# Attention and down-projection in 64-row tiles: one TensorE mode for scores and sums

## The chip, the cores and the metric

The kernel runs on one core of a Trainium2 chip. The metric is device time in microseconds (us) of one execution, the median of several runs. One execution was also taken with the hardware profiler; every line of a profile shown here comes from such an execution.

## What is computed

```
scores = z @ z.T / S                       # per batch, S = 3008, d_qk = 64
attn   = max(scores, 0) ** 2
x      = u * (attn @ v)                    # D = 256
h      = x @ w_in                          # 256 -> 2048
out    = (h * sigmoid(1.702 * h)) @ w_out  # 2048 -> 256
```

There are 8 batches of 3008 rows. Inputs and output are float32 in DRAM; the kernel computes in float16 with float32 sums.

## The kernel before

**Tiles.** A batch has 24 row blocks of 128 (NJ, the last one half full, 64 rows, called SREM) and six chunks (NCH) of 512 columns, the last one 448 wide. The transposed z (ZT) holds the 64 values of d_qk twice, on partitions 0 to 63 and on 64 to 127, so that two score matmuls of 64 rows can run side by side on the two halves of the array, each into its own PSUM bank.

**Scores.** `scores` handles units. A unit (i, jp) is two row blocks against one chunk: two 64-row matmuls into a two-bank PSUM tile sc (L198), one ScalarE activation (Relu, L210, or L207 for a narrow unit) to float16, one VectorE squaring (L224, L215, L208) into a tile a. Since scores are symmetric, units below the diagonal are not computed but taken from transposing DMAs on SP's queue (tt, ad; L230, L217). `take(b, n)` issues the next n units of a queue; the tables SCHED (batches 1 to 7), SCHED0 (batch 0) and TAIL say at which step of which chunk how many are taken, and units are made about one chunk before they are used. Units are taken in groups of three in most places.

**Attention.** `attend(b, i)` sums over 23 full row blocks and the half block for chunk i: o[c] += V[j, c].T @ a[j], for the two column halves c of D. Each step is a 128-row matmul of 512 columns (L281). Chunks 0 and 1 of batch 0 alternate between both c (`both`); all others do c = 0 first and then c = 1, with one half-block step, in which both c get a 64-row matmul, between them (or where AT says). When a sum is complete, `gate` multiplies it by the transposed u on VectorE (L290, into xt).

**Feed-forward.** `up_group` does two 128-row blocks of w_in: four matmuls into a two-bank tile hg (L314), gelu on ScalarE (L322), a scaling on VectorE (L323) into gt. `down(b, k, s, h)` does half of the 16 row blocks of w_out for 128 output rows: eight matmuls of 256 columns into yp (L337); after a pair of row blocks ScalarE evicts it (y, L343) and issues the store. 19 up groups (LAGY) are issued among the steps of chunks 4 and 5 (HEAD). The other 29 alternate with one `down` each; the remaining downs come last, and among them the score units of the next batch's chunk 0 (TAIL).

**Loads.** u comes in by four DMAs on GpSimd's queue per chunk (`load_u`, L168); the first waits until VectorE has transposed the chunk that had the buffer (`turn_u`, L175, at step 12 of a chunk, TURN). V comes in on SP's queue and is cast on GpSimd (L153); z of the next batch also goes through GpSimd (L129 to L132).

**Order and buffers.** The order of each engine's instructions is the order in which the program writes them; semaphores are set where data or buffers require it. [...] ps2 has 3 buffers of two banks (sc, hg, zp), ps1 has 2 of one bank (o, yp).

Of the kernel before, what the change touches and what calls it, by code (L numbers as in the profile page):

```python
# [9 lines left out]
F32 = mybir.dt.float32  # L10
F16 = mybir.dt.float16
P = 128
# [3 lines left out]
def kernel(  # L16
# [16 lines left out]
    B, S, D = u.shape  # L33
# [29 lines left out]
    pu = ctx.enter_context(tc.tile_pool(name="pu", bufs=2))  # L63
    pa = ctx.enter_context(tc.tile_pool(name="pa", bufs=1))
    pw = ctx.enter_context(tc.tile_pool(name="pw", bufs=2))
    ps2 = ctx.enter_context(tc.tile_pool(name="ps2", bufs=3, space=bass.MemoryType.PSUM))
    ps1 = ctx.enter_context(tc.tile_pool(name="ps1", bufs=2, space=bass.MemoryType.PSUM))
    ET = mybir.EngineType
    ctx.enter_context(tc.manual_schedule(engines={ET.PE, ET.Pool, ET.SP, ET.DVE, ET.Activation}))

# [3 lines left out]
    dve.memset(nil, 0.0)  # L74

    ZT, V16, UQ, UT, XT, unit, TT = {}, {}, {}, {}, {}, {}, {}

    def warm_up(n):

# [30 lines left out]

    def first_zt(g):
        z2 = ZT["st"][:, g * CB:(g + 1) * CB]
        zp = ps2.tile([P, CB, P], F16, name="zp", tag="ps2")
        for k in range(CB):
            pe.transpose(zp[:, k, :], z2[:, k, :, :], ident)  # L115
        zt = ZT[0][:, g * CB:(g + 1) * CB, :].rearrange("d n p -> d (n p)")
        nb = CB if g < NCH - 1 else CB - 1
        dst = zt[:, :nb * P].rearrange("d (p n) -> d n p", n=nb)
        if g == 0:
            act.activation(dst, zp[:, :nb, :], AF.Copy, scale=1.0)  # L120
        else:
            dve.tensor_copy(dst, zp[:, :nb, :])  # L122
        if nb < CB:
            dve.tensor_copy(zt[:, nb * P:], zp[:, nb, :])
# [124 lines left out]
        return TT[b, cj, i][:, :, g, :]  # L249


    def attend(b, i, both=False, at=0):


        n = width(i)
        js, cs = list(range(NJ - 1)), range(2)
        own = i * CB
        if b == 0 and i == 3:
            js = js[own:-CB + 1] + js[:own] + js[-CB + 1:]
        elif b and i < NCH - 2:  # L260
            js = js[own:own + 2] + js[own + CB:-CB + 1] + js[own + 2:own + CB] + js[:own] + js[-CB + 1:]
        if both:
            order = [(c, j) for j in js[:-CB] for c in cs] + [(c, j) for c in cs for j in js[-CB:]]
            order.insert(-CB, (None, NJ - 1))
        else:
            order = [(c, j) for c in cs for j in js]
            order.insert(NJ - 1 - at, (None, NJ - 1))
        first = [next(k for k, s in enumerate(order) if s[0] in (c, None)) for c in cs]
        final = [max(k for k, s in enumerate(order) if s[0] in (c, None)) for c in cs]
        acc = {}  # L270

        def step(k):
            half, j = order[k]
            a = weights(b, i, j)
            for c in cs:
                if half not in (c, None):
                    continue
                if k == first[c]:
                    acc[c] = ps1.tile([P, CH], F32, name="o", tag="ps1")
                h = slice(c * SREM, (c + 1) * SREM) if half is None else slice(0, P)  # L280
                pe.matmul(acc[c][:, :n], V16[b][h, j, c, :], a[h], start=k == first[c], stop=k == final[c])  # L281
            for c in cs:
                if k == final[c]:
                    gate(c)

        def gate(c):
            ut = UT[b, i][:, c].rearrange("p q t -> p (q t)")
            x = XT[b, i]
            if i < NCH - 1 or b % 2:
                dve.tensor_tensor(x[:, c, :n], acc[c][:, :n], ut[:, :n], ALU.mult)  # L290
            else:
                dve.tensor_tensor(x[:, c, :LFULL], acc[c][:, :LFULL], ut[:, :LFULL], ALU.mult)
                dve.tensor_tensor(XT[b + 1, i][:, c, LAST:], acc[c][:, LFULL:n], ut[:, LFULL:n], ALU.mult)

        XT[b, i] = XT.get((b, i)) or pa.tile([P, NCC, CH], F16, name="xt", tag="xt", bufs=8)
        if i == NCH - 1 and b % 2 == 0:
            XT[b + 1, i] = pa.tile([P, NCC, CH], F16, name="xo", tag="xo")
        return [lambda k=k: step(k) for k in range(len(order))]


    GT, Y = {}, {}

    def blocks(b):

        return [(i, CH if i < NCH - 1 or b % 2 else LFULL) for i in range(NCH)]
# [22 lines left out]
    def down(b, k, s, h):  # L328
# [12 lines left out]
        if h == 1 and (s % 2 == 1 or s == ns - 1):  # L341
            s0 = s - s % 2
            act.activation(Y[b, k][:, s0:s + 1, :], yp[:, :s % 2 + 1, :], AF.Copy, scale=1.0 / FSC)  # L343
        r0 = b * S + i * CH
        full = min(n, S - i * CH) // P
        final = b == B - 1 and k == NCH - 1
        if h == 1 and (s == ns - 1 or final and s % 2 == 1):
            s0 = s - 1 if final else 0
            act.dma_start(
                out[r0 + s0 * P:r0 + min(full, s + 1) * P].rearrange("(n p) c -> p n c", p=P),  # L350
                Y[b, k][:, s0:min(full, s + 1), :],
            )
        if h == 1 and s == ns - 1 and full < ns:
            for h_, bb in enumerate((b, b - 1)):
                (act if b == B - 1 else pool).dma_start(
                    out[bb * S + S0:(bb + 1) * S], Y[b, k][h_ * SREM:(h_ + 1) * SREM, full, :],
                )


    LAGY = 2 * NFG + 3  # L360
    HEAD = {NCH - 2: (14, 4), NCH - 1: (0, 4)}

    def pieces(b, i):

# [6 lines left out]
    def split(lst, sizes):  # L371
# [6 lines left out]

    TAIL = {3: 3, 7: 3, 11: 3, 15: 3}
    SCHED = {
        0: {4: 3, 16: 3, 28: 3, 40: 3},
        1: {8: 3, 23: 3},
        2: {8: 3, 23: 3},
        3: {23: 3},
        4: {8: 3},
        5: {},
    }
    AT = {0: -5, 4: NJ - 1 - 8}  # L390


    TURN = {(True, i): 12 for i in range(1, NCH - 1)}
# [3 lines left out]
    SCHED0 = {  # L397
        0: {0: 1, 6: 2, 14: 2, 22: 2, 30: 2, 38: 2},
        1: {0: 2, 8: 2, 15: 2, 22: 2, 30: 2, 38: 2},
        2: {0: 2, 8: 2, 23: 3, 34: 3},  # L400
        3: {8: 3, 23: 3},
        4: {1: 3, 12: 3, 23: 3},
        5: {0: 1},
    }
    AT0 = {4: NJ - 1 - 12}
    HEAD0 = {NCH - 2: (28, 4), NCH - 1: (2, 3)}

    queue = []

    def take(b, n):  # L410
        if n:
            group = [queue.pop(0) for _ in range(n)]
            scores(b, group)
# [22 lines left out]

    for b in range(B):
        nup = NCH * NFG
        sched, head_at, half_at = (SCHED, HEAD, AT) if b else (SCHED0, HEAD0, AT0)
        head = 0  # L440
        for i in range(NCH):
            for n, step in enumerate(attend(b, i, b == 0 and i < 2, half_at.get(i, 0))):
                if b == 0 and i == 0 and n == 5:
                    load_u(0, 0)
                if b == 0 and i == 0 and n in FIRST_ZT:
# [4 lines left out]
                    if k + 2 < NCH:  # L450
                        load_u(b, k + 2)
                take(b, sched[i].get(n, 0))
                h0, hn = head_at.get(i, (n + 1, 1))
                if head < LAGY and n >= h0 and (n - h0) % hn == 0:
                    up_group(b, head)
                    head += 1
                step()
# [18 lines left out]
        for q in range(head, nup):  # L476
# [4 lines left out]
            up_group(b, q)  # L481
            if q >= LAGY:
                down(b, *downs.pop(0))
        for n in range(len(downs)):
            if more:
                take(b + 1, TAIL.get(n, 0))
            down(b, *downs[n])


# [28 lines left out]
```

## Time and profile before

| | |
|---|---|
| median of 3 runs | 1251.93 us (1250.12 to 1258.75) |
| the profiled execution's own time | 1250.78 us |
| its span, first to last instruction | 1248.8 us |
| TensorE matmuls (PE) | 1239.4 us busy, 7575 matmuls |
| ScalarE (ACT) | 754.2 us busy |
| VectorE (DVE) | 628.5 us busy |
| GpSimd (POOL) | 233.3 us busy |
| granted TensorE clock | 1.000 over the span |

A line of the chain in order of time has the start in us, the length in us, the engine, the tile written, the line of the code and the number of instructions. A line of the timeline has start, length, engine, line, operation, tile written and tiles read, the shape (rows * columns of the weights for a matmul), the number of instructions that follow each other, and in brackets how long the engine was idle before and what ended that. PEld is TensorE's weight load; a q after an engine's name means its queue or sequencer. [...] matmuls that follow each other overlap in these rows; the distance between starts is what one costs.

### The profile page before, as it was taken

To read this page: it belongs to the slowest core of one execution; us is meant where nothing else is said; L and a number is where in the kernel's file an instruction comes from. 1 tells how busy PE (TensorE), PEld (TensorE's weight loads), DVE (VectorE), ACT (ScalarE), POOL (GpSimd) and SP (SyncE) were. 2 spreads that over 40 slices of the span, in tenths; PEclk is the share of its full clock that TensorE was granted. 3 is DMA by queue.
4 is the path that set the end of the run, shared out by engine and by line. 5 is a ranking of instruction groups with operands and counts; after the bars stand their busy time and mean duration, and the time that the engine had idled before them with its cause. 6 is when DMAs were issued, how large, how long until landed. Compare 5 with 4: busy or idle time off the path is not lost.

```text
span 1248.8 us, 19199 instructions
## 1 busy us (share of the span) xinstructions
PE 1239.4 (99%) x7575; PEld 682.6 (55%) x7575; DVE 628.5 (50%) x901; ACT 754.2 (60%) x829; POOL 233.3 (19%) x333
## 2 busy tenths in 40 slices
PE   8999999999999999999999999999999999999998
PEld 3345764466544675446754467444674446734566
DVE  7665445544455445554454544655445454464431
ACT  5776674566745667366673666745666456664663
POOL 4224202221022210223102230022211222000000
PEclk9999999999999999999999999999999999999999
DMA  9937279622886228852397524965239552493001
GB/s 229 185 66 171 71 167 181 126 68 69 186 167 127 69 85 191 162 106 68 95 192 155 106 76 99 205 130 107 98 102 197 120 113 84 117 196 74 1 35 68
DMA packets 370394, 151.75 MB, mean 122 GB/s; under 512 B 312864, under 2 KB 363936, under 8 KB 370304
## 3 DMA queue, kind: packets, MB, share of 16 engines
q1 hardware_dynamic: 311840, 96.38, 36.3%
q0 software_dynamic: 33440, 29.37, 12.0%
q10 hardware_dynamic: 25024, 24.78, 6.0%
q8 instruction: 59, 0.97, 0.3%
q14 instruction: 31, 0.25, 0.1%
HBM read 60.29 MB, written 24.64 MB: 68 GB/s over the span
## 4 chain that ended last, share of the span: by engine, by line
PE 97%; DVE 1%; issue 1%; ACT 1%; DMA 0%; SPq 0%; ACTq 0%; DVEq 0%
PE o L281 38%; PE yp L337 27%; PE hg L314 26%; PE sc L198 6%; DVE a L224 1%; ACT rl L210 0%; DMA zf<-in_z_dram 0%; DVE zst L109 0%; DVE ut L175 0%; DVE xt L290 0%; DVE ZT L122 0%; PE zp L115 0%; ACT y L343 0%; SPq L95 0%; ACTq L210 0%
## 5 line engine op out<-in xcount | busy, mean ns | idle before, releaser
L322 ACT ACTIVATE gf<-hg 128x1024 f32<-128x1024 f32 (+1 forms) x384 | 385.9, 1006 | 232.4 <-PE hg L314 221.5
L323 DVE TENSOR_SCALAR gt<-gf 128x1024 f16<-128x1024 f32 (+1 forms) x384 | 278.1, 725 | 326.7 <-ACT gf L322 324.4
L210 ACT ACTIVATE rl<-sc 128x1024 f16<-128x1024 f32 x311 | 299.5, 1025 | 161.2 <-PE sc L198 160.0
L337 PE MATMUL yp<-W,gt 128*128 128x256 f16 x3008 | 371.1, 273 | 0.0
L281 PEld LDWEIGHTS <-V 128*128 128x128 f16 (+1 forms) x2304 | 213.1, 98 | 280.0 <-issue 43.3
L314 PE MATMUL hg<-xt,W 128*128 128x512 f16 (+1 forms) x1408 | 354.6, 374 | 0.0
L337 PEld LDWEIGHTS <-gt 128*128 128x128 f16 x3008 | 292.1, 98 | 90.6 <-issue 11.1
L281 PE MATMUL o<-a,V 128*128 128x512 f16 (+2 forms) x1244 | 297.0, 373 | 0.8 <-DVE a L224 0.8
L224 DVE TENSOR_TENSOR a<-rl 128x1024 f16<-128x1024 f16 x276 | 192.2, 697 | 170.3 <-ACT rl L210 170.2
L168 POOL DMA_DIRECT2D uq<-in_u_dram x188 | 126.1, 678 | 629.0 <-DVE ut L175 619.3
L281 PE MATMUL o<-tt,V 128*128 128x512 f16 x920 | 219.0, 379 | 0.9 <-DVE xt L290 0.9
L314 PEld LDWEIGHTS <-W 128*128 128x128 f16 x1536 | 149.7, 98 | 125.6 <-issue 1.4
L153 POOL CAST V<-vst 128x512 f16<-128x512 f32 x96 | 67.9, 746 | 143.8 <-PE o L281 116.1
L198 PE MATMUL sc<-ZT 64*128 64x512 f16 (+1 forms) x692 | 93.4, 373 | 0.9 <-DVE ZT L122 0.8
L343 ACT ACTIVATE y<-yp 128x512 f32<-128x512 f32 x96 | 56.4, 588 | 50.8 <-PE yp L337 50.3
L290 DVE TENSOR_TENSOR xt<-o,ut 128x512 f16<-128x512 f32 x80 | 54.7, 685 | 36.7 <-PE o L281 36.7
L175 DVE STREAM_TRANSPOSE ut<-uq 128x1024 f32<-128x1024 f32 (+1 forms) x48 | 58.4, 1216 | 0.2
L198 PEld LDWEIGHTS <-ZT 64*128 64x128 f16 x692 | 24.1, 94 | 58.3 <-issue 45.7
L215 DVE TENSOR_TENSOR a<-rl 128x1024 f16<-128x1024 f16 x35 | 24.2, 692 | 45.2 <-ACT rl L210 44.9
L207 ACT ACTIVATE rl<-sc 128x512 f16<-128x512 f32 x35 | 20.9, 597 | 41.6 <-PE sc L198 41.6
L281 PE MATMUL o<-ad,V 128*128 128x512 f16 x140 | 41.6, 379 | 0.0
L314 PE MATMUL hg<-xo,W 128*128 128x512 f16 x128 | 32.8, 379 | 0.0
(28 smaller groups left out, 92.3 us busy)
## 6 DMA issues: line engine op xcount, KB each, us to landing
out_dram<-y ACTq DMA_DIRECT2D x40, 512.0 KB, 2.9
vst<-in_v_dram SPq DMA_DIRECT2D x39, 512.0 KB, 4.5
uq<-in_u_dram POOLq DMA_DIRECT2D x156, 128.0 KB, 2.9
tt<-a SPq DMA_TRANSPOSE x230, 3.2
uq<-in_u_dram POOLq DMA_DIRECT2D x32, 112.0 KB, 3.1
vst<-in_v_dram SPq DMA_DIRECT2D x8, 384.0 KB, 4.4
out_dram<-y ACTq DMA_DIRECT2D x7, 384.0 KB, 3.1
zst<-in_z_dram POOLq DMA_DIRECT2D x7, 368.0 KB, 6.0
```

The source lines that it names most:

```text
L153: pool.tensor_copy(V16[b][:, n0:n0 + VB, k, :].rearrange("p n (q c) -> p n q c", c=QW), vst.rearrange("p n (q k c) -> p n q k c", k=NCC, c ...
L168: eng.dma_start(uq[k * QW:(k + 1) * QW, :n // QW].rearrange("t q k c -> t q (k c)"), src[:, :, cs])
L175: dve.transpose(ut[:, :, :n // QW, :].rearrange("p k q t -> p q k t"), UQ.pop((b, i))[:, :n // QW])
L198: pe.matmul(sc[:, r, :m * P], zt[h, 2 * kp + r, :], zt[h, (qi + 1) * CB - m:(qi + 1) * CB, :], start=True, stop=True,)
L210: act.activation(rl, sc, AF.Relu, scale=csc)
L224: dve.tensor_tensor(a, rl, rl, ALU.mult)
L281: pe.matmul(acc[c][:, :n], V16[b][h, j, c, :], a[h], start=k == first[c], stop=k == final[c])
L314: pe.matmul(hg[:, e, :n], W1[:, c, ff * P:(ff + 1) * P], XT[b, i][:, c, :n], start=(c == 0), stop=(c == NCC - 1),)
L322: act.activation(gf[:, :, :n], hg[:, :, :n], AF.Gelu_apprx_sigmoid, scale=1.0 / FSC)
L323: dve.tensor_scalar(g, gf[:, :, :n], FSC, None, ALU.mult)
L337: pe.matmul(yp[:, s % 2, :], GT[b, k, ff // CB][:, ff % CB, s * P:(s + 1) * P], W2[:, ff, :], start=(ff == 0), stop=(ff == NFF - 1),)
L343: act.activation(Y[b, k][:, s0:s + 1, :], yp[:, :s % 2 + 1, :], AF.Copy, scale=1.0 / FSC)
```

## The change

- Attention of chunks 2 to 4 in batch 0 and of chunks 0 to 4 in all others no longer uses 128-row matmuls. Each step is a pair of 64-row matmuls: rows 0 to 63 of block j for c = 0 and rows 64 to 127 for c = 1, each into its own bank. After all blocks and the half step, the tiles swap: rows 0 to 63 go to c = 1 and rows 64 to 127 to c = 0. Chunk 5 stays with 128 rows, and its half step is now its first.
- The last two row chunks of the down projection (chunks 4 and 5, in all batches but the last) are done by the new `down64` in the same way: pairs of 64-row matmuls of 256 columns, each row tile at another block of output rows, then swapped. With four blocks of output rows it uses two PSUM tiles and one swap, with three (chunk 5 in batches 0, 2, 4, 6) three tiles and two swaps. All its y evictions come at its end.
- At each swap a bank passes from one row tile to the other. `post` puts a wait for the last pair on GpSimd's queue, and `behind` makes the next pair wait for that.
- Score units are taken one at a time, spread over the steps, two at the swap (step NJ).
- The 19 early up groups are all issued in chunk 5.
- PSUM: ps2 has 2 buffers and ps1 has 4; zp moves to ps1. The store becomes a function of its own.

```diff
-    ps2 = ctx.enter_context(tc.tile_pool(name="ps2", bufs=3, space=bass.MemoryType.PSUM))
-    ps1 = ctx.enter_context(tc.tile_pool(name="ps1", bufs=2, space=bass.MemoryType.PSUM))
+    ps2 = ctx.enter_context(tc.tile_pool(name="ps2", bufs=2, space=bass.MemoryType.PSUM))
+    ps1 = ctx.enter_context(tc.tile_pool(name="ps1", bufs=4, space=bass.MemoryType.PSUM))
...
+    TOP, LOW, FULL = slice(0, SREM), slice(SREM, P), slice(0, P)
+    def post(last):
+        sig = pool.nop()
+        for m in last:
+            tc.add_manual_dep(sig.ins, m.ins.name, SYNC, reason="row tiles of one bank")
+        return sig
+    def behind(sig, m):
+        tc.add_manual_dep(m.ins, sig.ins.name, SYNC, reason="row tiles of one bank")
...
+        half = [(0, TOP, NJ - 1), (1, LOW, NJ - 1)]
         if both:
-            order = [(c, j) for j in js[:-CB] for c in cs] + [(c, j) for c in cs for j in js[-CB:]]
-            order.insert(-CB, (None, NJ - 1))
+            order = [[(c, FULL, j)] for j in js[:-CB] for c in cs] + [[(c, FULL, j)] for c in cs for j in js[-CB:]]
+            order.insert(-CB, half)
+        elif i == NCH - 1:
+            order = [half] + [[(c, FULL, j)] for c in cs for j in js]
         else:
-            order = [(c, j) for c in cs for j in js]
-            order.insert(NJ - 1 - at, (None, NJ - 1))
+            order = [[(0, TOP, j), (1, LOW, j)] for j in js] + [half] + [[(1, TOP, j), (0, LOW, j)] for j in js]
...
+        acc, turn = {}, NJ if order[-1][0][1] != FULL else -1
         def step(k):
+            done = []
+            for m in order[k]:
+                c, h, j = m
+                if (k, m) == first[c]:
+                    acc[c] = ps1.tile([P, CH], F32, name="o", tag="ps1")
+                ins = pe.matmul(
+                    acc[c][:, :n], V16[b][h, j, c, :], weights(b, i, j)[h],
+                    start=(k, m) == first[c], stop=(k, m) == final[c],
+                )
+                if k == turn:
+                    behind(acc["sig"], ins)
+                done.append(ins)
+            if k == turn - 1:
+                acc["sig"] = post(done)
...
+    def down64(b, k):
+        ns = blocks(b)[k][1] // P
+        shift, per = (2, 2) if ns == CB else (1, 1)
+        order = [(s, (s + shift) % ns, ff) for s in range(ns) for ff in range(NFF)]
+        turns = [32] if ns == CB else [16, 32]
+        last = {s // per: n for n, o in enumerate(order) for s in o[:2]}
+        yp, sigs = {}, {}
+        def step(n):
+            s0, s1, ff = order[n]
+            done = []
+            for s, h in ((s0, TOP), (s1, LOW)):
+                new = s // per not in yp
+                if new:
+                    yp[s // per] = ps1.tile([P, 2, D], F32, name="yp", tag="ps1")
+                ins = pe.matmul(
+                    yp[s // per][:, s % per, :], GT[b, k, ff // CB][h, ff % CB, s * P:(s + 1) * P], W2[h, ff, :],
+                    start=new, stop=n == last[s // per],
+                )
+                if n in turns:
+                    behind(sigs[n], ins)
+                done.append(ins)
+            if n + 1 in turns:
+                sigs[n + 1] = post(done)
+            if n == len(order) - 1:
+                y = Y[b, k] = pw.tile([P, CB, D], F32, name="y", tag="y")
+                for m in range(ns // per):
+                    act.activation(y[:, m * per:(m + 1) * per, :], yp[m][:, :per, :], AF.Copy, scale=1.0 / FSC)
+                store(b, k, ns - 1)
...
-    HEAD = {NCH - 2: (14, 4), NCH - 1: (0, 4)}
+    HEAD = 2
-    TAIL = {3: 3, 7: 3, 11: 3, 15: 3}
+    TAIL = {1: {n: 1 for n in (3, 12, 44, 54)}, 2: {n: 1 for n in (4, 25, 34, 43)}}
     SCHED = {
-        0: {4: 3, 16: 3, 28: 3, 40: 3},
-        1: {8: 3, 23: 3},
-        2: {8: 3, 23: 3},
-        3: {23: 3},
-        4: {8: 3},
+        0: {n: 1 for n in (1, 4, 7, 11, 28, 30, 33, 36, 39, 43)} | {NJ: 2},
+        1: {n: 1 for n in (4, 9, 34, 40)} | {NJ: 2},
+        2: {n: 1 for n in (4, 9, 34, 40)} | {NJ: 2},
+        3: {n: 1 for n in (38,)} | {NJ: 2},
+        4: {n: 1 for n in (2,)} | {NJ: 2},
         5: {},
     }
...
-        2: {0: 2, 8: 2, 23: 3, 34: 3},
-        3: {8: 3, 23: 3},
-        4: {1: 3, 12: 3, 23: 3},
+        2: {n: 1 for n in (0, 3, 7, 11, 30, 34, 38, 42)} | {NJ: 2},
+        3: {n: 1 for n in (4, 9, 34, 40)} | {NJ: 2},
+        4: {n: 1 for n in (0, 3, 6, 9, 12, 32, 36)} | {NJ: 2},
         5: {0: 1},
...
+        if more:
+            while downs[0][0] < NCH - 2:
+                down(b, *downs.pop(0))
+            for k in range(NCH - 2, NCH):
+                turns, steps = down64(b, k)
+                at = {n: 3 - len(turns) for n in turns} | TAIL[len(turns)]
+                for n, step in enumerate(steps):
+                    take(b + 1, at.get(n, 0))
+                    step()
```

## The prediction

> **What bounds the kernel now.** I read the engine shares first, then the chain that ended last, then that chain in order of time, then ScalarE's, VectorE's and GpSimd's timelines of the same stretch.
>
> ```profile
> PE 1239.4 (99%) x7575; PEld 682.6 (55%) x7575; DVE 628.5 (50%) x901; ACT 754.2 (60%) x829; POOL 233.3 (19%) x333
> PE 97%; DVE 1%; issue 1%; ACT 1%; DMA 0%; SPq 0%; ACTq 0%; DVEq 0%
> ```
>
> TensorE is busy 99% of the span and is 97% of the chain, and no wait of it in the list of waits exceeds 1.2 us in total. So only TensorE's own slots count: what makes it stream less, or stand still. The chain in order of time shows what a slot is:
>
> ```profile
> 307.96 0.86 PE hg L314 x4
> 308.82 3.49 PE yp L337 x32
> ...
> 316.56 0.75 PE sc L198 x6
> 317.31 3.60 PE yp L337 x32
> ```
>
> Four 512-wide matmuls take 0.86, so 0.216 each; 32 of 256 take 3.49, so 0.109 each. Six score matmuls (64 rows, two row tiles side by side) are three pairs and should take 0.65; they take 0.75, and the 32 matmuls after them 3.60 instead of 3.49. So entering 64-row mode costs 0.10 and leaving it 0.11: 0.107 a switch. In the order of instructions I counted neighbours with different row counts: 262 switches before. 262 x 0.107 = 28 us is what the modes cost now.
>
> ```profile
> 345.08 2.86 ACT L210 ACTIVATE rl<-sc 128x1024 f16<-128x1024 f32 x3 [1.56 <-PE sc L198]
> ...
> 347.97 0.69 DVE L224 TENSOR_TENSOR a<-rl 128x1024 f16<-128x1024 f16 x1 [0.23 <-ACT rl L210]
> 348.58 1.24 DVE L175 STREAM_TRANSPOSE ut<-uq 128x1024 f32<-128x1024 f32 x1
> ...
> 348.75 0.82 PE L198 MATMUL sc<-ZT 64*128 64x512 f16 x6
> 349.18 2.85 ACT L210 ACTIVATE rl<-sc 128x1024 f16<-128x1024 f32 x3 [1.24 <-PE sc L198]
> ...
> 350.11 2.62 POOL L168 DMA_DIRECT2D uq<-in_u_dram  x4 [18.46 <-DVE ut L175]
> ```
>
> ScalarE starts 0.43 after a score unit's first matmul. Three evictions in a row take 2.86, one 1.02: they follow each other every 0.91, and a unit's PSUM is free about 0.06 after its own 1.02. The squaring starts 0.03 later, the transposition of u 0.61 after the squaring, the four DMAs for the next u 0.29 after its end.
>
> [...] here four such (zp, 17.86 to 18.08) took 0.22, so 55 ns. [...] it is a run of four.
>
> **The change, part by part**, against the profiled execution (1250.8; its span 1248.8).
>
> *Modes.* The streaming work stays: 128 rows in one matmul or two 64-row tiles in a pair take one slot. In the built order I count 46 switches. 216 x 0.107 = 23.1 us gained. The doubled loads and matmuls lie in the pair's slot: score pairs already load two tiles of weights under the preceding pair. 512-wide pairs give an instruction every 54 ns, as yp does now. The 832 pairs of 256 need one every 27 ns, zp's rate in a short run: I take 0.109. It cannot be less, since streaming fills it; at twice the rate seen per instruction in yp it would be 0.218 and cost 91 us.
>
> *Swap signals.* post() puts a wait for TensorE's last pair on GpSimd's queue and lets TensorE's next weight load wait for it. 56 are added: 38 in attention, 18 in down64. Where the queue is free the way there and back is short: a CAST on GpSimd is seen to start some 0.1 after the matmul it waits for ends. The matmul ends 0.38 after its start, 0.1 to GpSimd, 0.1 back and a load make 0.6; the two score units placed at the turn fill 0.22 + 0.43 = 0.65. Nothing. But GpSimd works in order, and in chunks 1 and 2 of batches 1 to 7 the signal stands behind the four u DMAs. Counting from the score unit at step 9:
>
> - VectorE: 0.43 + 1.02 + 0.03 (squaring) + 0.61 + 1.24 (transposition) + 0.29 = 3.62, first u DMA;
> - GpSimd's sequencer runs ahead of its engine, but not by four: in the two lines below (its timeline, and the rows of L129) four such DMAs begin at 229.38, and the semaphore wait that stands behind them ran at 230.8, 1.4 later. So 5.0, and 5.1 back at TensorE;
> - TensorE: 0.22 for the unit, 15 steps of 0.216, two units 0.43: it is there at 3.9.
>
> ```profile
> 229.38 2.70 POOL L168 DMA_DIRECT2D uq<-in_u_dram  x4 [12.58 <-DVE ut L175]
> ...
> L129 POOLq EVENT_SEMAPHORE  x1: 17/17/17, 230.8 to 230.8; - x1
> ```
>
> Stall 1.1 to 1.2, which nothing covers: TensorE waits in order, and all matmuls are behind. 14 x 1.15 = 16.1. In batch 0 chunk 3 is alike (1.15), and in chunk 2 the unit stands at step 11, two steps nearer: 1.6. Together 18.9. Before, the same DMAs were late too, but nothing stood behind them.
> In down64 with three row blocks (batches 0, 2, 4, 6) each of two swaps has one unit as cover: there at 0.109 + 0.216 = 0.33, back at about 0.5. 8 x 0.2 = 1.6. The other ten have two units: nothing. What else stands ahead of signals on GpSimd (the casts of V after chunk 5, the u DMAs of the up projections, the load of W2 before batch 0's chunk 4) is over microseconds earlier.
>
> *PSUM.* ps2 goes from three buffers to two, so a unit must wait for the eviction of the last but one. In chunk 0 (from step 24) units stand at 24, 24, 28, 30, 33, 36, 39, 43, with the first at 0 us:
> - evictions start at 0.43 and 1.34, end at 1.45 and 2.36;
> - step 28 is reached at 1.30 and waits to 1.51: 0.21. Step 30 is reached at 2.16 and waits to 2.42: 0.26. From there 0.87 lie between units against 0.91 for an eviction: 0.04 each, three times.
> So 0.6 a batch, 4.2 in all. Earlier in the chunk, the evictions of y (0.60, 0.42 for a 256-wide one) and the out DMA (0.38 on ScalarE's queue) now come together at the end of down64, just ahead of the units at steps 1, 4 and 7. Odd batches before it: the y pair and the DMA keep ScalarE from 0.31 to 1.85 after the last pair, the unit of step 1 is out at 2.87, step 7 wants its buffer at 2.06: 0.9, three times. Even ones, about 0.3, four times. 4.0.
> ps1 has four buffers, but down64 with three blocks takes one more tile, so chunk 0's second accumulator gets the bank of the block's first y. ScalarE still evicts the unit of step 43 (0.43, next start 1.34), then y (0.42): free at 1.8, wanted at five steps of 0.109 + 0.22 = 0.76. 1.04 x 4 = 4.1.
>
> *Order.* Chunk 5 now begins with its half step, and in batch 0 that needs the unit issued at the same step: 0.43 + 1.02 + 0.03 + 0.69 + 0.05 = 2.2 against 0.2, so 2.0 lost once; the 0.9 of waits of o for xt goes, since o has four buffers. 1.1. Up heads in chunk 5: one each 2 or 3 steps of 0.189 plus 0.86, at least 1.24; ScalarE needs 1.0 for each: hidden, with 0.2 to spare. SP's transposes keep their order; VectorE's work is the same.
>
> Sum: 18.9 + 1.6 + 8.2 + 4.1 + 1.1 = 33.9 lost, 23.1 gained: +10.8, so 1261.6 against the profiled execution. The median of the runs shown is 1.1 above that execution; I say 1262.
>
> **Rivals.**
> A. *The signal passes early.* If GpSimd's sequencer takes all four DMAs at once, the signal goes at about 3.7 and the 18.9 vanish: 1262 - 19 = 1243. For it: only the wait for the transposition is certain to hold the queue. Against: the 1.4 us at L129.
> B. *Issue bounds the 256-wide pairs.* Rate per instruction: 27 ns wanted; 0.130 a pair gives 832 x 0.021 = 17 more, 1279[...]. It decides from 0.112 on. For: no long run at this rate in the trace. Against: zp.
> C. *Modes win outright.* Not slower: the signals cost nothing and the evictions keep pace, as they do with three buffers now, so the 23.1 stand against some 6 left (the accumulator, down64's swaps): 1234. For: ScalarE is busy 60%. Against: the two-buffer ledger. It decides where signal stalls and unit waits together fall under 10.
> D. *The mode is not what it seems:* loads of a 64-row tile show in attention too. At 10 ns for each of the 1788 pairs in attention +18: 1280. Against: three score pairs in 0.65.
>
> **How the numbers follow.** Forecast 0.60, A 0.12, B 0.18, C 0.05, D 0.05. The forecast's own range is 1252 to 1270: the signals from 12 (they pass a DMA earlier) to 24[...], PSUM 8 to 16. Down to A and to B's first value it is 1243 to 1279. A measurement of this kernel tells about 1% from no change, so 1239.4 and 1264.4 are the bounds. Faster: C, little of A: 0.06. Slower: B, D and a third of the forecast's range: 0.42. Within: 0.52.
>
> **What would show it.** After: waits of o's weight load for GpSimd of 1.1 to 1.2 us, some 16 of them, the chief new wait; sc waiting for rl in chunk 0; o waiting for y in four batches; yp pairs at 0.109; nearly no gap of 0.1 around sc. Pairs above 0.115, or no waits for GpSimd, would prove me wrong.

## The result, and the profile after

| | before | after |
|---|---|---|
| median | 1251.03 us (1249.97 to 1258.75) | 1267.8 us (1265.19 to 1271.47) |
| the profiled execution's own time | 1250.78 us | 1269.06 us |
| its span | 1248.8 us | 1267.3 us |

The ratio is 1.0126, with a 95% interval of 1.0083 to 1.0168: 1.3% slower. The forecast was 1262, slower with a chance of 0.42 and within 1% with 0.52. Engine shares and the chain that ended last, after:

```profile
PE 1228.4 (97%) x10155; PEld 707.5 (56%) x10155; DVE 623.1 (49%) x901; ACT 762.8 (60%) x833; POOL 233.9 (18%) x333
PE 87%; ACT 4%; DVE 2%; POOL 2%; DMA 2%; issue 2%; ACTq 0%; DVEq 0%; SPq 0%
```

The span grew by 18.5 us while TensorE's busy time fell by 11.0. TensorE was 97% of the chain before and is 87% now: the mode switches went, and waits for every other engine came. The mode part of it, in the chain in order of time:

```profile
163.52 0.43 PE yp L403 x6
163.95 0.22 PE sc L211 x2
164.17 0.98 PE yp L403 x18
```

This is where down64 begins. Six matmuls of 256 columns in pairs are three slots of 0.109 and would take 0.33; the row gives 0.43, as it holds the one change from 128 to 64 rows. The score pair behind it takes 0.22, its slot, and the 18 matmuls (nine pairs) after it 0.98, again 0.109 each: nothing is added on the way in or back. So a score unit between 64-row pairs costs its slot and no switch.

The waits of TensorE, after (total, number, longest, in us; PEld is the weight load that runs ahead, so the line of PE is the time that the matmuls lost):

```profile
PEld L294 <- POOLq L83: 29.6, 38, 2.1
...
PE o L294 <- POOLq L83: 18.7, 16, 1.7
...
PE sc L211 <- ACT rl L223: 3.4, 4, 0.9
PE o L294 <- ACT y L415: 3.0, 4, 0.8
PE o L294 <- DVE a L237: 2.5, 2, 1.8
PE o L294 <- DMA ad<-a: 2.4, 1, 2.4
```

All are new but a part of those for DVE's a (one of 0.8 stood there before). The list subtracts the overlap with the matmul before, and leaves out waits shorter than that. So for the ledger below I took every matmul's start and compared it with where its slot would have let it start (the start before it, plus 0.216 or 0.109). Such delays sum to some 36.5 us before and 55 after; the difference is that of the spans.

One of the signals, in the timeline of chunk 1 of batch 1:

```profile
195.02 0.40 PE L211 MATMUL sc<-ZT 64*128 64x512 f16 x2
...
197.11 1.24 DVE L188 STREAM_TRANSPOSE ut<-uq 128x1024 f32<-128x1024 f32 x1
...
198.47 0.61 PE L211 MATMUL sc<-ZT 64*128 64x512 f16 x4
198.65 2.57 POOL L181 DMA_DIRECT2D uq<-in_u_dram  x4 [46.74 <-PE o L294]
...
200.10 1.68 PE L294 MATMUL o<-a,V 64*128 64x512 f16 x14 [1.01 <-POOLq L83]
```

The score unit at step 9 starts at 195.02. The first DMA of u begins 3.63 later and TensorE goes on 5.08 later; the forecast had 3.62 and 5.1. The four DMAs take until 201.22 on GpSimd's engine, yet TensorE is released at 200.1: GpSimd's sequencer does run ahead of its engine, but not by four: at 0.64 each the third was under way.

What ScalarE's work costs TensorE in the same batch, in two stretches of the timeline: first the start of chunk 0, just behind batch 0's down64 with three blocks, then chunk 0 behind its swap:

```profile
178.32 0.38 PE L294 MATMUL o<-a,V 64*128 64x512 f16 x1
179.00 0.96 ACT L415 ACTIVATE y<-yp 128x256 f32<-128x256 f32 x3
...
179.45 0.37 PE L294 MATMUL o<-a,V 64*128 64x512 f16 x1 [0.76 <-ACT y L415]
```

```profile
187.15 0.39 PE L211 MATMUL sc<-ZT 64*128 64x512 f16 x2
187.36 0.61 PE L294 MATMUL o<-a,V 64*128 64x512 f16 x4
188.06 0.39 PE L211 MATMUL sc<-ZT 64*128 64x512 f16 x2
188.28 0.82 PE L294 MATMUL o<-a,V 64*128 64x512 f16 x6
188.98 0.39 PE L211 MATMUL sc<-ZT 64*128 64x512 f16 x2
```

The first matmul of chunk 0's first pair starts at 178.32; its partner, which needs the bank of the first y, has to wait until ScalarE has evicted that and starts 1.11 late. Behind the swap, units start every 0.91, which is ScalarE's pitch and not TensorE's: three steps and a unit are 0.87, and with two steps in between (187.36, four matmuls) a unit is held 0.26.

Two things the forecast did not have. A transposing DMA was late twice, by 0.9 us in batch 0 and by 2.5 in chunk 3 of batch 4:

```profile
683.49 1.46 PE L294 MATMUL o<-a,V 64*128 64x512 f16 x12
687.31 0.61 PE L294 MATMUL o<-ad,V 64*128 64x512 f16 x4 [2.36 <-DMA ad<-a]
```

And after the wait for the half step in batch 0 (timeline; then the chain; then a stretch of it, whose seventh column is the granted clock):

```profile
82.75 0.38 PE L211 MATMUL sc<-ZT 64*128 64x512 f16 x2
...
84.23 0.69 DVE L237 TENSOR_TENSOR a<-rl 128x1024 f16<-128x1024 f16 x1
...
84.98 0.66 PE L294 MATMUL o<-a,V 64*128 64x448 f16 x3 [1.84 <-DVE a L237]
```

```profile
85.64 1.62 PE hg L335 x4
...
91.24 0.86 PE hg L335 x4
```

```profile
85.60:89.00 3.40, 3.40 (x10) 1.22 (x8) 0.65 (x1) 1.02 (x1) 0.00 (x0) 0.50 0.00 0
```

TensorE stood still for 2.0 us, and from 85.6 on it was granted half its clock for 3.4 us: the same four matmuls take 1.62 and, later, 0.86.

### The profile page after: what moved, and what is told of

It reads as the page before. It is cut to its first block, busy times and chain, and to the rows that moved or that the text cites. A ratio compares the mean times of both kernels' runs of the same rounds, so it can differ in the third digit from the quotient of the medians.

```text
span 1267.3 us, 24406 instructions
## 1 busy us (share of the span) xinstructions
PE 1228.4 (97%) x10155; PEld 707.5 (56%) x10155; DVE 623.1 (49%) x901; ACT 762.8 (60%) x833; POOL 233.9 (18%) x333
## 3 DMA queue, kind: packets, MB, share of 16 engines
q8 instruction: 79, 1.29, 0.5%
## 4 chain that ended last, share of the span: by engine, by line
PE 87%; ACT 4%; DVE 2%; POOL 2%; DMA 2%; issue 2%; ACTq 0%; DVEq 0%; SPq 0%
PE o L294 32%; PE hg L335 26%; PE yp L358 19%; PE yp L403 6%; PE sc L211 4%; ACT rl L223 3%; POOL uq L181 2%; DVE ut L188 1%; ACT y L415 1%; DMA ad<-a 1%; DMA W<-in_moe_w_in_dram 1%; DVE a L237 1%; DMA uq<-in_u_dram 1%; DVE zst L122 0%; ACTq L376 0%
## 5 line engine op out<-in xcount | busy, mean ns | idle before, releaser
L294 PEld LDWEIGHTS <-V 64*128 64x128 f16 (+1 forms) x4052 | 227.0, 94 | 282.5 <-POOLq L83 29.6
L294 PE MATMUL o<-a,V 64*128 64x512 f16 (+2 forms) x2010 | 320.0, 373 | 22.8 <-POOLq L83 17.3
L358 PE MATMUL yp<-W,gt 128*128 128x256 f16 x2176 | 275.5, 273 | 0.0
L358 PEld LDWEIGHTS <-gt 128*128 128x128 f16 x2176 | 212.9, 98 | 70.7
L294 PE MATMUL o<-tt,V 64*128 64x512 f16 (+1 forms) x1762 | 210.4, 376 | 2.2 <-POOLq L83 1.5
L211 PE MATMUL sc<-ZT 64*128 64x512 f16 (+1 forms) x692 | 122.2, 370 | 5.0 <-ACT rl L223 3.4
L403 PE MATMUL yp<-W,gt 64*128 64x256 f16 x1664 | 103.9, 269 | 0.0
L403 PEld LDWEIGHTS <-gt 64*128 64x128 f16 x1664 | 80.5, 94 | 19.9 <-POOLq L83 4.0
L364 ACT ACTIVATE y<-yp 128x512 f32<-128x512 f32 x68 | 40.4, 594 | 32.7 <-PE yp L358 32.2
L294 PE MATMUL o<-ad,V 64*128 64x512 f16 x280 | 42.8, 376 | 2.4 <-DMA ad<-a 2.4
```

What stands on the lines that cost most here:

```text
L211: pe.matmul(sc[:, r, :m * P], zt[h, 2 * kp + r, :], zt[h, (qi + 1) * CB - m:(qi + 1) * CB, :], start=True, stop=True,)
L294: ins = pe.matmul(acc[c][:, :n], V16[b][h, j, c, :], weights(b, i, j)[h], start=(k, m) == first[c], stop=(k, m) == final[c],)
L358: pe.matmul(yp[:, s % 2, :], GT[b, k, ff // CB][:, ff % CB, s * P:(s + 1) * P], W2[:, ff, :], start=(ff == 0), stop=(ff == NFF - 1),)
L403: ins = pe.matmul(yp[s // per][:, s % per, :], GT[b, k, ff // CB][h, ff % CB, s * P:(s + 1) * P], W2[h, ff, :], start=new, stop=n == last[ ...
```

## The experiments

All were timed against the kernel before. Its median was 1249.72 for e1 to e4, 1250.54 for e5 to e8, 1251.32 for e9 to e11 and 1250.87 for e12.

**One cause at a time.** e1 issues the DMAs of u behind the swap's signal:

```diff
                     turn_u(b, k)
-                    if k + 2 < NCH:
+                    if k + 2 < NCH and i < 2 and b == 0:
                         load_u(b, k + 2)
+                if n == NJ + 1 and (b > 0 or i > 1):
+                    k = i + (b > 0)
+                    if (b == 0 or 0 < i < NCH - 1) and k + 2 < NCH:
+                        load_u(b, k + 2)
```

> The changed kernel with one edit: the four u DMAs of a chunk are issued at step 25, behind the swap's signal on GpSimd's queue, instead of at step 12, ahead of it. Theory 1 (signals are held by the u DMAs): the 16 waits of o for GpSimd that the changed kernel's trace shows, 21.4 us in all, go to under 1 us, and the time falls from 1267.8 by 20 to 22, to about 1246-1248. Theory 2 (the way to GpSimd and back is slow in itself, or GpSimd is slow to answer for another reason): at least half of the 21 stays, 1257 or more. Theory 3 (the late u loads only move the wait): a new wait of VectorE's transposition for u, and less than 10 gained.

Measured: 1260.03 us (1256.26 to 1266.85), ratio 1.0088 [1.0053, 1.0124]. Its waits and, in chunk 3 of batch 1, its timeline:

```profile
PE o L294 <- DMA ad<-a: 7.9, 5, 2.3
PEld L294 <- POOLq L83: 6.5, 38, 0.2
```

```profile
212.16 1.27 SPq L230 DMA_TRANSPOSE ad<-a  x1
...
217.39 0.61 PE L294 MATMUL o<-ad,V 64*128 64x512 f16 x4 [1.58 <-DMA ad<-a]
```

The attention's signals cost nothing any more: the longest wait of a load for one is 0.2, and no matmul of attention starts late for it, against 21.4 us after. So the queueing behind u's DMAs is their whole price. But only about half of it came back: 11.4 us between the profiled executions, 7.8 between the medians (the intervals of the two ratios overlap). The delays for transposing DMAs grew from 3.4 us to about 12, with five of the waits for ad in chunk 3, and the mean granted clock of the profiled execution is 0.994, against 0.998 after.

e2 spreads the units of chunk 0, e3 gives down64 with three blocks an early first y, e4 makes batch 0's last unit a chunk earlier:

```diff
-        0: {n: 1 for n in (1, 4, 7, 11, 28, 30, 33, 36, 39, 43)} | {NJ: 2},
+        0: {n: 1 for n in (1, 7, 11, 15, 19, 31, 35, 39, 43, 46)} | {NJ: 2},
```

```diff
-        shift, per = (2, 2) if ns == CB else (1, 1)
+        shift, per = (2, 2) if ns == CB else (2, 1)
...
+            if ns < CB and n == last[0]:
+                y = Y[b, k] = pw.tile([P, CB, D], F32, name="y", tag="y")
+                act.activation(y[:, :per, :], yp[0][:, :per, :], AF.Copy, scale=1.0 / FSC)
```

```diff
-        4: {n: 1 for n in (0, 3, 6, 9, 12, 32, 36)} | {NJ: 2},
-        5: {0: 1},
+        4: {n: 1 for n in (0, 3, 6, 9, 12, 15, 32, 36)} | {NJ: 2},
+        5: {},
```

> The changed kernel with one edit: in chunk 0 of batches 1 to 7 the score units stand at steps 1, 7, 11, 15, 19, 24, 24, 31, 35, 39, 43, 46 instead of 1, 4, 7, 11, 24, 24, 28, 30, 33, 36, 39, 43, so at least four steps (1.08 us) apart where ScalarE needs 0.91 for each. Theory 1 (two buffers in ps2 with ScalarE's pace make the waits of sc for rl, 9.8 us of which about 9 lie in chunk 0): those fall to under 2, the time by about 7 to 8, to 1260. Theory 2 (units are late because ScalarE starts late after down64, whatever the spacing): the waits at the first units stay, about 4 gained. Theory 3: units issued later make attention of chunk 1 wait for them, and nothing is gained.

> The changed kernel with one edit: with three output row blocks, down64 pairs block s with s+2 instead of s+1, so that the first block's sum is complete at step 31 and its y is evicted there instead of at the end. Theory 1: the wait of chunk 0's second accumulator for y (4 times 1.11 us) goes, but the units of steps 1 to 7 now run into ScalarE's remaining y and out DMA a microsecond earlier, so most comes back as waits of sc for rl: 0 to 1.5 us gained, 1266.5 to 1268. Theory 2 (the waits are independent): 4.4 us gained, 1263.5.

> The changed kernel with one edit: in batch 0 the last score unit is taken at step 15 of chunk 4 (one more unit there) instead of at step 0 of chunk 5, whose first step, the half step, needs it. Theory 1: the wait of 2.0 us goes, and with it the 3.4 us of half clock that follow it in the changed kernel's trace (about 1.8 us of lost streaming): 3.5 to 4 us gained, 1264. Theory 2 (the clock dip has another cause): the wait goes, the dip stays, 2 us gained, 1265.8.

| | median, us | ratio | what the trace shows |
|---|---|---|---|
| e2 | 1258.73 (1253.62 to 1268.23) | 1.0082 [1.0047, 1.0117] | delays of sc for ScalarE 9.8 to 1.5 us |
| e3 | 1266.92 (1265.86 to 1272.8) | 1.0136 [1.0119, 1.0153] | o waiting for y 4.4 to 0; sc for ScalarE 9.8 to 13.9 |
| e4 | 1263.26 (1261.94 to 1271.99) | 1.0123 [1.0089, 1.0157] | the 2.0 us wait gone (o waiting for DVE's a 2.5 to 0.5); mean granted clock 0.997, against 0.998 after |

By the medians e2 is 9.1 and e4 4.5 us below the changed kernel, about what their terms were. The intervals of these ratios overlap that of the changed kernel, so it is the traces, not the times, that show it. The half clock does not follow the wait that e4 removes in every execution: in e10 the same wait stands (o for DVE's a, the longest 1.8, as after), and the mean granted clock is 1.000. e3 removed its term and got it back in the next one: the first y was still evicted ahead of the same units. The y and the units of chunk 0 share ScalarE, and a cure for the y alone only moves the wait.

**Why is ad late?** e1 left two answers: u's DMAs, which now run beside the transposes, slow them; or ad is late by its own place in SP's queue, and the signals' waits had hidden that. e5 takes the other way out of the signal problem, u first; e6 keeps e1's way and changes ad's place.

```diff
-    TURN = {(True, i): 12 for i in range(1, NCH - 1)}
-    TURN |= {(False, i): (38, 28)[i] if i < 2 else 12 for i in range(NCH)}
+    TURN = {(True, i): 2 if i < 3 else 12 for i in range(1, NCH - 1)}
+    TURN |= {(False, i): (38, 28, 2, 2)[i] if i < 4 else 12 for i in range(NCH)}
```

> The changed kernel with one edit: the transposition of u and the four u DMAs behind it move from step 12 to step 2, in the chunks whose swap they held up (chunks 1 and 2 of batches 1 to 7, 2 and 3 of batch 0). In the previous experiment, where the DMAs went behind the swap, the signals' waits went from 21.4 us to nothing, but 12 us of waits of o for transposed tiles (ad, tt) came instead, and 8 to 10 us were gained. Theory 1 (the u transfers, moved to step 25, slowed the ad transposition that chunk 3 needs; moved ahead, they are over by then): signals under 1 us and DMA waits of o at most 4 us, as in the changed kernel: 1246 to 1250. Theory 2 (ad is late by its own place, step 24, once the stalls that hid it are gone): signals under 1, but ad waits of about 1 to 2 us in most batches, 1253 to 1260.

```diff
-        if i == NCH - 1 or b == 0:
+        if i in (3, NCH - 1) or b == 0:
             return lst
```

> The kernel with the u DMAs at step 25, with one more edit: chunk 3's units are taken in their plain order, so the unit whose upper half is transposed into ad is made at step 4 of chunk 2 instead of step 24, four microseconds earlier. Theory 1 (ad was late because of the u transfers beside it): the early ad is clear of them, the ad waits of chunk 3 (9 us) go, about 1249 to 1252 (batch 0's wait for tt stays). Theory 2 (late by its place): the same here; the two differ in the kernel with u first. Theory 3 (SP's queue is behind by more than four us): waits stay, 1258.

e5: 1253.75 us (1245.0 to 1264.27), 1.0023 [1.0, 1.0046]. The signals cost nothing here either, and ad is late in chunk 3 just the same, 0.4 to 3.1 us in six of seven batches. With u's DMAs some 20 steps away it is not they. Its interval lies clear of the changed kernel's (1.0083 to 1.0168), so that the times, too, show what the place of u's DMAs costs. e6: 1257.64 us (1245.21 to 1263.32), 1.0034 [1.001, 1.0059]. ad is in time, and the tt that its move put last is late instead:

```profile
PEld L294 <- DMA tt<-a: 10.1, 7, 2.9
PE o L294 <- DMA tt<-a: 8.7, 6, 2.4
```

**All at once, and the price of the modes.** e7 has e2, e3, e4, e5 and e6's order of chunk 3. e8 is e7 with attention back in 128-row matmuls, c after c, and no signal in it; the units stay single, so that it has 456 switches instead of 46.

> The changed kernel with five edits together: u first (step 2), units of chunk 0 spread, first y early, the half step's unit early in batch 0, and ad's unit early. If the waits are what they were taken for, and none takes their place: signals 21, sc for rl 8, y 4, half step and clock dip 4, ad about 2.5: 38 to 40 us off 1267.8, 1228 to 1232, faster than the kernel before by 1.5 to 1.8%. A rival: DMA waits of o take part of it, as before with the u DMAs late: 1236 to 1242. If it ends above 1250, 64-row mode is no gain at all.

```diff
-            order = [[(0, TOP, j), (1, LOW, j)] for j in js] + [half] + [[(1, TOP, j), (0, LOW, j)] for j in js]
+            order = [[(0, FULL, j)] for j in js] + [half] + [[(1, FULL, j)] for j in js]
```

> The kernel with all five edits, but attention in 128-row matmuls again, first all of c = 0, the half step, then all of c = 1 (no signals in attention); the single units stay where they are, so each costs two switches: 456 switches in the built order against 46. At 0.107 us a switch: 43.9 us slower than the kernel with all edits, less about 1 us of waits that the slower pace hides: 1271 to 1275. If a switch costs less where only one unit stands between (a rival), or part of the price was PSUM waits, under 30 us slower. If the doubled loads of 64-row mode cost something in attention, the difference is smaller than 43 by that.

e7: 1249.3 us (1236.3 to 1261.76), 0.997 [0.995, 0.999]. e8: 1272.44 us (1269.58 to 1281.17), 1.0175 [1.0135, 1.0215]. For e7, 1228 to 1232 was expected. The waits of the forecast's ledger are gone but for some 2 us of sc for ScalarE; what is left is some 16 us of waits for transposing DMAs, most of it in one line:

```profile
PE o L294 <- DMA tt<-a: 11.7, 10, 2.2
```

The timeline of SP in batch 1, and what TensorE does at its end:

```profile
162.31 16.28 SPq L243 DMA_TRANSPOSE tt<-a  x10
178.68 1.22 SPq L230 DMA_TRANSPOSE ad<-a  x1
180.00 12.21 SPq L243 DMA_TRANSPOSE tt<-a  x8
192.31 1.25 SPq L230 DMA_TRANSPOSE ad<-a  x1
193.66 8.68 SPq L243 DMA_TRANSPOSE tt<-a  x6
202.44 1.48 SPq L230 DMA_TRANSPOSE ad<-a  x1
204.01 7.56 SPq L243 DMA_TRANSPOSE tt<-a  x4
```

```profile
208.63 2.77 PE L294 MATMUL o<-tt,V 64*128 64x512 f16 x24
213.33 1.04 PE L294 MATMUL o<-tt,V 64*128 64x512 f16 x8 [1.93 <-DMA tt<-a]
```

From 162.3 to 211.6 SP does nothing but issue transposes, 31 of them, with hardly a gap. An undisturbed one takes 1.26 and the next follows at 1.35; with the disturbed ones the mean is 49.3 / 31 = 1.59. Set against the ends of the squarings that feed them, their issue falls behind from 0.1 at the first to 7.2 us at the ad at 192.31. The chunk's last tt was issued at 209.60, landed 3.7 later, and was wanted 1.9 before that. The kernel before has the same queue at the same pace (29 of them from 163.7 to 209.2, so 1.57 each) and falls behind by up to 5.9; its TensorE came later. That can be read off the time between the landing of a transposed tile and its first use. Of the 140 tiles that are transposed behind the first 100 us, 1 had less than 0.5 us before, 19 have in e7, and none in e8, where attention takes TensorE longer. So what the change uncovers, once its own waits are mended, is the next limit behind TensorE.

e8 shows the same from the other side. Its 410 more switches are seen one by one:

```profile
176.54 1.47 PE L294 MATMUL o<-a,V 128*128 128x512 f16 x6
177.94 0.28 PE L211 MATMUL sc<-ZT 64*128 64x256 f16 x2
178.16 1.04 PE L294 MATMUL o<-a,V 128*128 128x512 f16 x4
```

Six slots of 0.216 would end at 177.84; the score pair starts at 177.94 (0.10), and the next 128-row matmul 0.22 after it where the pair of 256 is 0.109 long (0.11). In sum its delays at switches are 47 us, 0.10 each, against 7 in e7. But at the slower pace its waits for transposing DMAs are 1.8 us against some 16: 40 lost, 15 given back, 25 net; the medians differ by 23.1. That e8's time fell into the expected 1271 to 1275 is luck: e7 was some 19 us slower than expected, and the difference between the two is little more than half of the 43 expected.

**Is it the place in the queue?** e9 gives chunk 3 the order ad, turned pair (the tt that the chunk itself needs), rest. e10 is that order and e5's edit alone, without the other mends. e11 takes e9 and moves the two units from the swap to two steps behind it, which bares the signal.

```diff
-        if i in (3, NCH - 1) or b == 0:
+        if i == NCH - 1 or b == 0:
             return lst
-        k = max(len(lst) - 6, 0)
+        k = max(len(lst) - 6, 2 * (i < NCH - 1))
```

> All edits of e7, but chunk 3's units of batches 1 to 7 are queued as 6, 7 (its ad), 10, 11 (the turned pair), 8, 9 instead of 6, 7, 8, 9, 10, 11. In e7's trace (batch 1) the turned pair's tt of chunk 3 was squared at 205.85 and 207.36, issued by SP 2.4 and 2.2 us later, and used at 213.33 after a wait of 1.93: it is the last but two of some 30 transposes in SP's queue, and of about 17 us of waits for transposing DMAs some 12 stand at this place, one in each of seven batches. Theory 1 (place in SP's queue): with the turned pair two places ahead its squares come 24 steps (5 us) earlier, so these 12 us go; ad keeps its place; a median of 1249.3 - 12 = about 1237, 1233 to 1241, and a smaller spread from run to run. Theory 2 (SP's queue as a whole is the pace, 32 transposes at 1.35 us and more, a lag of up to 7 us behind the squares): the waits come out elsewhere (ad of chunk 3, or tt of chunk 2), and the median stays at 1246 to 1250.

> The changed kernel with two edits only: the DMAs of u and their transposes at step 2 instead of 12 (e5), and chunk 3's units of batches 1 to 7 queued as ad, turned pair, rest (e9). e5 had about 11 us of o waiting for transposing DMAs in its profile, 9.8 of it ad in chunk 3, and 1253.75. Theory 1: ad is computed with units 1 and 2 instead of 3 and 4 of the chunk, 15 steps (3.2 us) earlier, and its waits of 0.4 to 3.1 go, while the turned pair is still in time: 1243 to 1246. Theory 2 (SP's queue as a whole): the waits move to the turned pair, 1250 to 1254. What is left in either case is that of sc for ScalarE (9.8), y (4.4) and the half step (2.0 and the clock behind it).

```diff
-        1: {n: 1 for n in (4, 9, 34, 40)} | {NJ: 2},
+        1: {n: 1 for n in (4, 9, 34, 40)} | {NJ + 2: 2},
```

(and so in every table entry that has NJ)

> e9 with the two score units of each swap moved two steps behind it (step 26 instead of 24), so that nothing stands between the signal's matmul and the first o matmul in the other row half: prices GpSimd's round trip without cover, in 38 swaps. From the changed kernel's trace the bare round trip is some 0.35 to 0.6 us from the matmul's start, of which the matmul and the one beside it cover 0.2: 38 x 0.2 to 0.4 = 8 to 15 us more than e9. If the prediction's pricing is wrong and the signal costs nothing without u's DMAs beside it: within 2 us of e9.

e9: 1243.16 us (1236.46 to 1248.01), 0.9928 [0.9901, 0.9955]. The waits in chunk 3 fell from 13.5 us to 3.1, much as theory 1 said, but the gain is half of what it said. The formula also turned round the four units of chunk 4, which I had not meant; there o now waits in all seven batches, 0.87 in six and 1.43 in one. And batch 0 had one wait of 4.1 us in this execution:

```profile
42.80 0.38 PE L294 MATMUL o<-tt,V 64*128 64x512 f16 x2
47.15 1.46 PE L294 MATMUL o<-tt,V 64*128 64x512 f16 x6 [3.97 <-DMA tt<-a]
```

Here too the clock follows: six matmuls (three slots, 0.65 and a tail) take 1.46.

e10: 1255.65 us (1248.42 to 1265.93), 1.0033 [1.0011, 1.0055], where 1243 to 1246 was expected by one theory and 1250 to 1254 by the other. In its profiled execution (1251.1) ad is in time and the delays for transposing DMAs are 8.2, of which 6.7 are chunk 4's; the unmended terms stand as before (sc 10.5, y 4.4, half step 2.0). That explains about 1250. That half of its executions were slower than this by 4.6 us and more, no profile of mine shows; it stays open.

e11: 1257.45 us (1249.56 to 1260.84), 1.0045 [1.0021, 1.0068]. Waits of the load for a signal, in e9 and in e11:

```profile
PEld L294 <- POOLq L83: 5.6, 31, 0.4
```

```profile
PEld L294 <- POOLq L83: 23.2, 38, 0.9
```

23.2 over 38 is 0.61 for a load that would otherwise have run ahead; the matmul itself starts 0.28 late, in 36 of 38 within 0.01, so 10.9 us in all. The medians differ by 14.3. So a bare signal costs 0.28 net, and the two score units cover it whole.

**The last mend.** e12 is e9 with chunk 4's order back, and with the two loads of W1 in batch 0 one chunk later, since SP's transposes took up to 5.8 us each beside them.

```diff
-        k = max(len(lst) - 6, 2 * (i < NCH - 1))
+        k = max(len(lst) - 6, 2 * (i < NCH - 2))
...
-                if i < 2:
+                if 0 < i < 3:
...
-                    for k in range(2 * i, 2 * i + 2):
+                    for k in range(2 * i - 2, 2 * i):
```

> e9 with two edits. (a) Chunk 4's four units of batches 1 to 7 go back to the changed kernel's order, 10, 11, 8, 9: in e9 they were 8, 9, 10, 11 by the same formula, and o waited 0.87 us at chunk 4's end in all seven batches for a tt issued 5.35 us before its use (6.1 to 6.7 us in all, with one of 1.43). (b) The two halves of W1, which GpSimd loads behind chunks 0 and 1 of batch 0 (29.6 and 42.9 us), are loaded behind chunks 1 and 2: in e9 SP's transposes of batch 0 took up to 5.8 us each from 31 to 57 us beside these loads, lagged up to 17.7 us behind their squares, and o waited 4.1 us once. Theory (place and pace of SP's queue): 1243.16 - 6.1 - 0 to 4 = 1233 to 1237, the profile's waits for tt in chunk 4 and in batch 0 gone. Rival for (a): ad, which then comes last, is late instead and the median stays at 1241 to 1244. Rival for (b): W1 comes too late for the first up groups of batch 0, with a wait for it at 90 to 100 us.

e12: 1236.66 us (1231.93 to 1250.15), 0.9892 [0.985, 0.9933]. It is the fastest kernel here, 31 us below the changed one and 1.1% below the one before. The two intervals of e9 and e12 overlap, so the step between them is not shown by the times alone. The profiled execution is one of the two slowest of six (1249.5); in it chunk 4's waits of batches 1 to 7 are gone, but some 12 us of waits for transposing DMAs are left elsewhere (3.5 for tt in batch 0, 4.5 in chunk 2 of batch 5, 2.3 in chunk 3 of batch 7). And the rival for (b) came true in another form than I had named it:

```profile
59.38 0.64 POOL L181 DMA_DIRECT2D uq<-in_u_dram  x1 [0.53 <-DMA W<-in_moe_w_in_dram]
```

W1 itself is in time, but a DMA of u on the same queue waits for W1's transfer, and a swap's signal stands behind it: o, due at 60.7, starts 3.0 us late. The long transposes moved with the loads, too, and take up to 9.7 us there. So part (b) only moved the trouble, and (a) is what I would keep; the two were not timed apart.

## Why the prediction came out as it did

The forecast was right in direction and about right in size: its steps were there, at the places that it named, and two terms it had not. By its own steps, each with the delay that the trace after shows at that place:

| step of the prediction | predicted, us | measured, us |
|---|---|---|
| modes, 262 to 46 switches | -23.1 | -22.8 (delays of the first start behind a switch 27.6 before, 6.9 after; of the one behind that 2.5 and 0.5) |
| signals behind the DMAs of u, 16 | +18.9 | +21.4 |
| signals in down64 with three blocks | +1.6 | +0.5 |
| units waiting for ScalarE, chunk 0 | +8.2 | +9.8 |
| o waiting for y's bank | +4.1 | +4.4 |
| half step of batch 0, net | +1.1 | +1.1 (2.0 of wait) |
| transposing DMAs late | not named | +3.4 |
| half clock behind the 2.0 us wait | not named | +1.7 |
| sum | +10.8 | +19.5; the span grew by 18.5 |

The measured column counts waits that have small counterparts before; it comes out 1.0 above the growth of the span.

- *Swap signals.* Right in mechanism, place and number: 16 waits, in chunks 1 and 2 of batches 1 to 7 and chunks 2 and 3 of batch 0. Most are 1.18 to 1.29 instead of 1.15, and 1.18 and 1.62 in batch 0. Two of 1.80 and 1.83 stand where the four DMAs did not run in one piece. e1 and e5 show that they are all u's DMAs, so rival A was wrong. The 1.4 us of run-ahead, read from one semaphore row, carried this step; in the trace after, the signal of the example passes GpSimd 1.35 behind the first DMA.
- *Down64's signals.* The step took the return at 0.5 where one unit covers 0.33, so 0.2 each; it is 0.06 (8 x 0.061). Over-sized by three.
- *PSUM.* The waits at steps 28 and 30 were forecast as 0.21 and 0.26 and are 0.21 and 0.27; the odd batches' 0.9 is 1.04 to 1.10, the even ones' 0.3 is 0.45 to 0.47. y's 1.04 is 1.11. e2 and e3 show that they are ScalarE's order of work, since moving the units or the y moves the waits.
- *Modes.* 0.107 a switch is right, seen again in e8 (0.10 in, 0.11 out). The start behind a switch is late by 0.096, the next one by another 0.01, and both together give nearly the forecast's 23.1.
- *Rivals B and D.* Pairs of 256 columns hold 0.109 for whole blocks, and 64-row loads cost nothing beside a pair (seven pairs of 512 from 681.98 to 683.49, so 0.216 each, the slot of one 128-row matmul before); B's price would have been 17 us and more, and none of it is there.
- *Rival C.* It said that the change wins outright if signals and evictions cost little. e12 reaches 1236.7 against C's 1234, but only after six other things were moved.
- *What was not priced.* The sum is short by 3.4 of transposing DMAs and 1.7 of clock. "SP's transposes keep their order" was true and was the wrong question: they had up to 5.9 us of backlog before, and the time they had left depended on how late TensorE was. A wait of 2.0 was followed by 3.4 us at half the clock. The prediction costed such waits at their own length.

That the forecast of 1262 came within 6 us of 1267.8 is not luck of cancelling terms of size: the over-sized ones (modes 0.3, down64 1.1) and the under-sized ones (signals 2.5, ScalarE 1.6, y 0.3, DMAs 3.4, clock 1.7) all are small against the 23 and 34 that were set against each other. The chances were the weaker part: 0.52 stood on "within 1%" with a forecast that was itself 0.9% slower.

## What to carry to other kernels

When a change takes time out of the bounding engine, write down for every queue behind it how far it lags and how much slack its last item has; that slack is about what can be gained before the queue is the bound. A semaphore through an in-order queue cost here what stood ahead of it on that queue (21.4 us for 16 behind u's DMAs) and little else (0.28 us each in e11, nothing under cover), so put it where the queue is empty, or do that queue's work first. Mend waits in sets that share an engine: e3 alone gained nothing, and much of what e1 removed went to the next late DMA.

## What the runs showed of the hardware

- A stall of TensorE can cost more than its length. What the matmuls just behind seven stalls took, from the timelines, against the same matmuls at full clock (0.86 for four of hg; for o 0.216 a pair and 0.17 for the tail of the last):

| stall | its length, us | matmuls behind it | they took, us | at full clock, us |
|---|---|---|---|---|
| e9, tt, batch 0 | 4.1 | 6 of o | 1.46 | 0.81 |
| e12, tt, batch 0 | 3.5 | 6 of o | 1.46 | 0.81 |
| e5, ad, chunk 3 of batch 4 | 3.1 | 4, then 32 of o | 0.61, then 5.32 | 0.60, then 3.63 |
| after, ad, chunk 3 of batch 4 | 2.5 | 4, then 32 of o | 0.61, then 3.63 | 0.60, then 3.63 |
| e7, tt, chunk 3 of batch 1 | 2.1 | 8 of o | 1.04 | 1.03 |
| after, half step | 2.0 | 3 of o, then 4 of hg | 0.66, then 1.62 | hg 0.86 |
| e1, ad, chunk 3 of batch 1 | 1.8 | 4, then 12 of o | 0.61, then 1.47 | 0.60, then 1.47 |

  In the trace after, the granted clock is 0.50 from 85.60 to 89.01, behind the 2.0 us, and 1.00 from 687.3 to 690.3, behind the 2.5. So the length alone does not decide whether half the clock follows; what does, these runs do not show. The one stretch after lasts 3.41 us and so costs 1.7.
- DMA transposes left SP at one per 1.35 us where nothing disturbed them (e7), at 1.59 on the mean in the stretch of e7 above, and at up to 5.8 (e9) and 9.7 (e12) beside the loads of W1. In that stretch of e7 they landed 2.3 to 6.6 us after issue. A second queue for them was not tried.
- GpSimd as a relay between two matmuls, with its queue empty, cost 0.28 us of TensorE's time (e11), and nothing where 0.43 us of other matmuls stood in between (e9).
